# Attention and MLP on one core: a block takes the first 512 tokens of one batch, and the last block takes all eight 64-token tails

## The chip, the cores and the metric

One core of a Trainium2 chip runs the whole program. The metric is the device time of one execution in microseconds (us). Before the change it is 324.11 us (median of 3 runs, 323.73 to 324.36). The profile is of one execution; its span (322.6 us) leaves out about 1.7 us that the device time has.

Engine names: PE is TensorE (PEld its weight loads), DVE is VectorE, ACT is ScalarE, POOL is GpSimd, SP is SyncE, which issues most DMAs.

## The reference, cut to what matters

```python
# q, k, v: [8 batches, 8 heads, 576 tokens, 64]
scores = scale * q @ k^T;  ret = scores * Dmat          # causal, decay gamma_h ** (i - j)
x = (ret @ v) -> [8 * 576, 512]                         # tokens in order: 576 of batch 0, 576 of batch 1, ...
h = x @ w_in                                            # [4608, 2048]
g = 0.5 * h * (1 + tanh(c * (h + 0.044715 * h**3)))
return g @ w_out                                        # [4608, 512], float32
```

## The kernel before

A batch has 576 tokens: four chunks of 128 and a **tail** of 64. Attention is done chunk by chunk with a running state; its output lands in `xT`. The MLP (the two layers with `w_in` and `w_out`) works on **blocks** of 512 tokens, nine in all. Before the change, block t takes tokens 512t to 512t+511 of the running order, so block 1 needs the tail of batch 0, then 448 tokens of batch 1. The MLP's second layer is sixteen matmuls for each of four 128-token tiles in block 0, and in later blocks seven half-size products (a Strassen-like scheme, `prod`) with sums by VectorE (`act_sums`; the sums of the weights are `weight_sums`). Attention work for the next block is put between the MLP's steps at places written by hand: `at(block, step, work)`. Every engine runs its instructions in the order written. A **cast** is the copy of a loaded float32 tile to 16 bits (with a scaling for q and k); a **turn** is its transpose. TensorE writes its results to PSUM, a memory of eight banks. The code is cut ("..."), and most comments in it are mine.

```python
    def load_tail(b):                       # six small DMAs issued by POOL, 384 KB
        for key in "kqv":
            for u in range(2):
                load(b, key, NC, u)
...
    def turn_dma(b):                        # batches from NPE on: transposed by DMA
        a = att[b]
        for key in "kq":
            nc.sync.dma_start_transpose(out=a["t" + key], in_=a[key])
...
        def send(o, i):                     # output of a block: 128 rows, two tiles
            nc.sync.dma_start(
                out=out[TB * t : TB * t + TB, :].rearrange("(u i p) d -> p u i d", u=2, i=2)[:, :, i, :], in_=o
            )
...
        elif m == 4:
            if last:                        # the last two stores: 128 rows in one piece each
                add(keep["o1"][:, u, 0:HD], keep["s1"][:, u], pr("B")[:, u])
                r0 = TB * t + 256 * u + 128
                nc.sync.dma_start(out=out[r0 : r0 + 128, :], in_=keep["o1"][:, u])
...
    at(0, -4, lambda: load_tail(0))                                  # tail 0 inside block 0
    at(0, 8, lambda: [cc(0, key, NC, P) for key in "kqv"])           # its casts, on POOL
    for p in range(HP):
        at(0, 15 + p, lambda p=p: turn_q4(1, p, (A.copy, V.tensor_copy)[p % 2]))
    at(0, 19, lambda: turn(0, NC, A.copy))
...
        if t == 0:                          # second layer of block 0: two passes over w_out, two banks each
            for i0, tags in ((0, "AB"), (2, "CA")):
                ...
```

## Time and profile before

| | before |
|---|---|
| device time, median | 324.11 us |
| span of the profile | 322.6 us |
| TensorE busy | 305.2 us (95%) |
| last VectorE add ends; span ends 3.3 us later | 319.33 us |

The profile by stretches comes first. Each row has a start and an end in us from the span's start, its length, then busy us and number of instructions for each engine, the granted TensorE clock (1.00 is full), the share of the 16 DMA engines' time that is busy, and GB/s. The cuts are where TensorE starts the first layer of blocks 1, 2, 3 and 8.

```profile
36.00:62.40 26.40, 21.83 (x178) 10.56 (x175) 17.26 (x28) 8.06 (x16) 16.75 (x21) 1.00 1.10 238
62.40:99.40 37.00, 35.14 (x406) 28.74 (x405) 29.40 (x49) 23.00 (x46) 25.82 (x31) 1.00 1.11 221
99.40:134.60 35.20, 34.19 (x334) 22.27 (x332) 21.72 (x43) 18.71 (x37) 18.45 (x26) 1.00 0.99 192
134.60:292.00 157.40, 157.40 (x1415) 99.86 (x1414) 84.05 (x181) 84.15 (x162) 35.58 (x45) 1.00 0.54 111
292.00:322.60 30.60, 26.36 (x178) 17.07 (x175) 10.36 (x23) 10.72 (x18) 0.00 (x0) 1.00 0.18 70
```

TensorE has no gap in blocks 3 to 7 (row 4). It stands 4.6 us in the rest of block 0 (row 1), 1.9 us in block 1, 1.0 us in block 2. Row 1 also has a DMA share above 1: the queues are full. Who is waited for there is shown by the chain of waits (start, length, what; each piece is what released the next):

```profile
36.40 8.59 DMA ld<-in_q_dram
...
45.07 1.05 POOL cq L223
...
48.15 1.06 POOL ck L232
49.20 1.02 POOL cq L232
50.22 0.80 POOL cv L221
51.03 1.00 POOL ck L232
52.03 0.56 POOL cv L221
```

Batch 1's q arrives late (45 us), then POOL casts one tile after another. The three casts from 48.15 to 51.02 us are tail 0's.

### The profile page before, as it was taken

How to read it: one execution, taken by the hardware profiler on the slowest of the kernel's cores; microseconds unless marked ns; L12 is line 12 of the kernel's file. 1: busy time of each engine (PE TensorE's matmuls, PEld its weight loads, DVE VectorE, ACT ScalarE, POOL GpSimd, SP SyncE). 2: the span in 40 equal slices, each digit the busy share in tenths (PEclk: the TensorE clock that was granted, in tenths of full speed). 3: DMA queues.
4: the chain of work that ended last, by engine and by line, in shares of the span. 5: the costliest groups of instructions: out<-in, count | busy, mean ns of one | idle time of the engine just before them, and what ended most of it. 6: DMA issues, size and time to landing. Idle time of an engine off the chain costs nothing.

```text
span 322.6 us, 6913 instructions
## 1 busy us (share of the span) xinstructions
PE 305.2 (95%) x2785; PEld 199.3 (62%) x2785; DVE 183.6 (57%) x367; ACT 167.2 (52%) x322; POOL 124.9 (39%) x179
## 2 busy tenths in 40 slices
PE   6889967998999999999999999999999999999994
PEld 2458624676786458745864586458646864685483
DVE  5853467897874667564647463754467446633341
ACT  6466322696643665365537654665376237614700
POOL 8679339966754409600960096009100000000000
PEclk9799999999999999999999999999999999999999
DMA  8999999999999978995599689900820030003003
GB/s 197 223 347 384 291 271 216 208 247 250 197 202 205 206 202 158 201 197 166 127 218 183 194 152 200 236 2 3 185 93 0 2 131 2 2 0 130 2 0 132
DMA packets 123472, 51.31 MB, mean 159 GB/s; under 512 B 111920, under 2 KB 113968, under 8 KB 123440
## 3 DMA queue, kind: packets, MB, share of 16 engines
q1 hardware_dynamic: 121904, 47.72, 66.9%
q0 software_dynamic: 1536, 3.15, 4.6%
q8 instruction: 22, 0.36, 0.5%
q14 instruction: 10, 0.08, 0.1%
HBM read 36.70 MB, written 9.44 MB: 143 GB/s over the span
## 4 chain that ended last, share of the span: by engine, by line
PE 74%; DMA 10%; DVE 6%; SPq 4%; issue 2%; POOL 2%; ACT 1%; DVEq 0%; POOLq 0%
PE hp L389 31%; PE opB L476 13%; PE opC L476 9%; PE opA L476 8%; DMA ld<-in_moe_w_out_dram 4%; DMA ld<-in_moe_w_in_dram 3%; PE xs L337 3%; PE st L288 3%; SPq L90 3%; DMA ld<-in_q_dram 3%; PE us L307 2%; PE xs L355 2%; PE tr L262 1%; DVE ret L294 1%; DVE wt L447 1%
## 5 line engine op out<-in xcount | busy, mean ns | idle before, releaser
L389 PE MATMUL hp<-xT,w_in_sb 128*128 128x512 f16 x448 | 103.8, 379 | 0.0
L395 ACT ACTIVATE gT<-hp 128x512 f16<-128x512 f32 x112 | 67.1, 599 | 61.5 <-PE hp L389 61.1
L389 PEld LDWEIGHTS <-w_in_sb 128*128 128x128 f16 x448 | 41.6, 98 | 44.3 <-issue 0.5
L294 DVE TENSOR_TENSOR ret<-st,cm 128x512 f16<-128x512 f32 x64 | 41.2, 685 | 35.9 <-PE st L288 35.8
L476 PEld LDWEIGHTS <-gT 128*128 128x128 f16 x512 | 49.3, 98 | 7.5 <-issue 0.7
L476 PEld LDWEIGHTS <-s 128*128 128x128 f16 x384 | 36.6, 98 | 5.2 <-issue 0.5
L328 ACT CAST tbd<-ws 64x256 f16<-64x256 f32 x64 | 25.8, 403 | 24.6 <-DVE ws L323 23.9
L232 POOL TENSOR_TENSOR ck<-ld,sc 128x512 f16<-128x512 f32 x31 | 33.2, 1071 | 11.5 <-DMA ld<-in_k_dram 6.8
L476 PE MATMUL opB<-wt,gT 128*128 128x256 f16 x256 | 31.4, 273 | 0.5 <-DVE ost L490 0.5
L406 PE MATMUL hp<-xT,w_in_sb 128*128 128x256 f16 x256 | 30.3, 273 | 1.5 <-ACT gT L412 0.7
L476 PE MATMUL opA<-w_out_sb,gT 128*128 128x256 f16 x256 | 30.8, 273 | 0.0
L458 DVE TENSOR_TENSOR s<-gT 128x512 f16<-128x512 f16 x32 | 14.6, 456 | 25.9 <-ACT gT L395 24.9
L634 POOL COPY gate<-s 128x1 f16<-128x1 f16 x4 | 0.8, 188 | 69.5 <-DVE s L461 69.5
L406 PEld LDWEIGHTS <-w_in_sb 128*128 128x128 f16 x256 | 24.4, 98 | 5.1 <-POOL w_in_sb L532 1.5
L232 POOL TENSOR_TENSOR cq<-ld,sc 128x512 f16<-128x512 f32 x24 | 25.9, 1078 | 0.1
L412 ACT ACTIVATE gT<-hp 128x512 f16<-128x512 f32 x32 | 18.9, 596 | 9.5 <-PE hp L406 9.3
L490 DVE TENSOR_TENSOR ost<-k,opC 128x512 f32<-128x512 f32 x16 | 11.0, 687 | 18.4 <-PE opC L476 18.1
L376 ACT CAST xT<-xs 128x512 f16<-128x512 f32 x31 | 18.1, 583 | 2.0 <-PE xs L355 1.0
L288 PE MATMUL st<-tt 64*128 64x128 f16 x288 | 15.6, 221 | 3.3 <-DVE tt L266 1.4
L490 DVE TENSOR_TENSOR k<-k,opB 128x512 f32<-128x512 f32 x16 | 10.9, 683 | 12.7 <-PE opB L476 12.6
L288 PEld LDWEIGHTS <-tt 64*128 64x128 f16 x288 | 8.5, 95 | 15.5 <-issue 10.9
L337 PEld LDWEIGHTS <-cv 128*64 128x64 f16 x288 | 9.4, 110 | 13.9 <-issue 12.5
(87 smaller groups left out, 387.8 us busy)
## 6 DMA issues: line engine op xcount, KB each, us to landing
out_dram<-ost SPq DMA_DIRECT2D x17, 512.0 KB, 3.3
ld<-in_q_dram SPq DMA_DIRECT2D x32, 256.0 KB, 5.1
ld<-in_k_dram SPq DMA_DIRECT2D x32, 256.0 KB, 5.8
ld<-in_v_dram SPq DMA_DIRECT2D x32, 256.0 KB, 5.6
ld<-in_moe_w_in_dram SPq DMA_DIRECT2D x16, 256.0 KB, 5.8
ld<-in_moe_w_out_dram SPq DMA_DIRECT2D x16, 256.0 KB, 5.7
lt<-in_k_dram POOLq DMA_DIRECT2D x16, 64.0 KB, 4.9
lt<-in_q_dram POOLq DMA_DIRECT2D x16, 64.0 KB, 5.9
```

The lines of the kernel that those rows point to most:

```text
L232: eng.tensor_tensor(out=dst.rearrange("p (h d) -> p h d", d=D), in0=raw.rearrange("p (h d) -> p h d", d=D), in1=sc[:, s0 : s0 + nh].unsque ...
L288: nc.tensor.matmul(st[hl][:, 128 * p : 128 * p + 128], a["tk"][r, 4 * c + p, :], tq(b, c, p)[r], start=True, stop=True)
L294: nc.vector.tensor_tensor(out=r[:, 0:w], in0=st[hl][:, 0:w], in1=m.rearrange("p n i -> p (n i)"), op=ALU.mult)
L328: cp(out=tbd[b % 2][r, c, :, r], in_=att[b]["w"][r])
L337: nc.tensor.matmul(xs[64 * hl : 64 * hl + 64, 128 * p : 128 * p + 128], a["v"][:, col(c, p, hl)], a["ret"][c, hl][:, 128 * p : 128 * p + 128],
L376: nc.scalar.copy(out=xT[:, g0 : g0 + 2], in_=src)
L389: nc.tensor.matmul(hp.rearrange("p (g t) -> p g t", t=TL), w_in_sb[:, ct, 128 * fc : 128 * fc + 128], xT[:, o : o + TB // TL, ct, :], star ...
L395: nc.scalar.activation(out=gT[t][:, fc].rearrange("p i n -> p (i n)"), in_=hp, func=AF.Gelu_apprx_tanh)
L406: nc.tensor.matmul(hp[:, 256 * x : 256 * x + 256].rearrange("p (g t) -> p g t", t=TL), w_in_sb[:, ct, 128 * (f + x) : 128 * (f + x) + 128] ...
L412: nc.scalar.activation(out=gT[t][:, f : f + 2, 2 * u : 2 * u + 2, :].rearrange("p f i n -> p f (i n)"), in_=hp.rearrange("p (f n) -> p f n ...
L476: nc.tensor.matmul(op[tag][:, HD * u : HD * u + HD], lhs(f), rhs[:, f], start=(new and u == 0 and f == 0), stop=(f == NH - 1), skip_group_ ...
L490: nc.vector.tensor_tensor(out=o, in0=a, in1=b, op=ALU.add)
```

## The change

The intent: keep tail 0 out of the crowded blocks 0 and 1. Block b takes tokens 0 to 511 of batch b; block 8 takes the eight tails. So each tail may be done at any time before block 8, and its states (`tbt`) and turned operands (`ett`) are kept apart. The second layer of block 0 uses four PSUM banks, so that the second half can begin before all of w_out has come. Batch 3 is transposed by DMA and no longer by TensorE, all tails by TensorE, and from batch `HOLD` on the loads are held back until the transposes have been issued. The diff, cut to its core (comments mine):

```diff
-    NPE = 4
+    NPE = 3
+    HOLD = 3
...
         def send(o, i):
-            nc.sync.dma_start(
-                out=out[TB * t : TB * t + TB, :].rearrange("(u i p) d -> p u i d", u=2, i=2)[:, :, i, :], in_=o
-            )
+            if t < B:
+                nc.sync.dma_start(
+                    out=out[S * t : S * t + TB, :].rearrange("(u i p) d -> p u i d", u=2, i=2)[:, :, i, :], in_=o
+                )
+                return
+            for v in range(2):
+                end(o[:, v], i, v)
+        def end(o, i, v):
+            b = 4 * v + 2 * i
+            nc.sync.dma_start(out=out.rearrange("(b s) d -> b s d", s=S)[b : b + 2, M0:S, :], in_=o)
...
-                r0 = TB * t + 256 * u + 128
-                nc.sync.dma_start(out=out[r0 : r0 + 128, :], in_=keep["o1"][:, u])
+                end(keep["o1"][:, u], 1, u)
...
-    at(0, -4, lambda: load_tail(0))
-    at(0, 8, lambda: [cc(0, key, NC, P) for key in "kqv"])
-    at(0, 11, lambda: weight_sums(0))
+    at(0, 23, lambda: weight_sums(0))
     for p in range(HP):
-        at(0, 15 + p, lambda p=p: turn_q4(1, p, (A.copy, V.tensor_copy)[p % 2]))
-    at(0, 19, lambda: turn(0, NC, A.copy))   # and tail 0's score, av, put at 21, 24, 25
+        at(0, (20, 21, 22, 24)[p], lambda p=p: turn_q4(1, p, A.copy))
-    TU = [(0, 21), (0, 25), (0, 29), (1, 1)]          # batch 1: casts and turn in one place
+    CU = [(0, 6), (0, 7), (0, 30), (1, 0)]            # casts on their own, earlier
+    TU = [(0, 24), (0, 28), (0, 32), (1, 1)]
...
+    PLAN = {1: (8, 13, 18, 23), 2: (9, 14, 19, 24), ...}             # four chunks of batch t+1 in block t
+    TAILS = {0: ((1, 10), (2, 0), (2, 4)), 1: ((2, 5), (3, 0), (3, 4)), ..., 7: ((7, 3), (7, 10), (7, 14))}
...
-            for i0, tags in ((0, "AB"), (2, "CA")):
+            tags = ("A", "B", "C", "hp")
+            for i0, f0, f1 in ((0, 0, 12), (2, 0, 8), (0, 12, 16), (2, 8, 16)):
```

More of the change, by code (lines that the diff above doesn't have):

```diff
@@ L40 @@
     NH = NF // 2
-    W = NC * 512 + 256
+    W = NC * 512
     NB = W // 128
-    RX = 1536
-    NPE = 4
+    NPE = 3
     LD = 16
@@ L58 @@
     ctx.enter_context(tc.manual_schedule())
-    BUFS = {"hp": 2, "att": 3, "A": 1, "B": 1, "C": 1}
+    BUFS = {"hp": 2, "t0": 1, "t1": 1, "t2": 1, "A": 1, "B": 1, "C": 1}
+    turns = {"n": 0}
     def bank(tag, name, dt=F32):
+        if tag == "att":
+            tag = "t" + str(turns["n"] % 3)
+            turns["n"] += 1
         return ps.tile([128, 512 if dt == F32 else 1024], dt, tag=tag, name=name, bufs=BUFS[tag])
@@ L121 @@
         seq += body(b)
-    q_ld = {"next": 0, "free": LD}
+    q_ld = {"next": 0, "free": LD, "hold": False}
     def pump(freed=0):
         q_ld["free"] += freed
-        while q_ld["next"] < len(seq):
+        while q_ld["next"] < len(seq) and not q_ld["hold"]:
             s = seq[q_ld["next"]]
@@ L194 @@
     for i in range(2):
-        t = const.tile([128, NC, HP, 128], F16, name=f"tbd{i}")
-        tbd.append(t)
+        tbd.append(const.tile([128, NC - 1, HP, 128], F16, name=f"tbd{i}"))
+    tbt = [const.tile([128, HP, 128], F16, name=f"tbt{i}") for i in range(3)]
     w_in_sb = const.tile([128, 4, DF], F16, name="w_in_sb")
     w_out_sb = const.tile([128, NF, DM], F16, name="w_out_sb")
-    xT = const.tile([128, RX // TL, HP, TL], F16, name="xT")
+    GM, GT = 2 * (TB // TL), 2 * (TB // TL)
+    xT = const.tile([128, GM + B, HP, TL], F16, name="xT")
     def filler(n, tag="C"):
@@ L210, in new_casts, with new_tail, act_of, turned @@
             a[key] = sb.tile([128, W], F16, tag="c" + key, name="c" + key, bufs=2)
+    def new_tail(b):
+        a = att[b]
+        for key in "kqv":
+            a["e" + key] = sb.tile([128, 256], F16, tag="e" + key, name="e" + key, bufs=2)
+        a["ett"] = sb.tile([128, 2, 2, 128], F16, tag="ett", name="ett", bufs=2)
+    def act_of(b, key, c):
+        return att[b][key if c < NC else "e" + key]
+    def turned(b, c):
+        return (att[b]["tt"], 4 * c) if c < NC else (att[b]["ett"], 0)
     def cast(b, key, c, eng):
@@ L215, in cast @@
         raw = a["raw"].pop((key, c))[:, 0:w]
-        dst = a[key][:, 512 * c : 512 * c + w]
+        o = 512 * c if c < NC else 0
+        dst = act_of(b, key, c)[:, o : o + w]
         if key == "v":
@@ L260, in turn @@
             for i in range(n):
-                o = 512 * c + 128 * i
+                o = (512 * c if c < NC else 0) + 128 * i
                 nc.tensor.transpose(
-                    t[:, 128 * (n * y + i) : 128 * (n * y + i) + 128], a[key][:, o : o + 128], ident
+                    t[:, 128 * (n * y + i) : 128 * (n * y + i) + 128], act_of(b, key, c)[:, o : o + 128], ident
                 )
         m = len(keys)
+        d, o = turned(b, c)
         copy(
-            out=a["tt"][:, 0:m, 4 * c : 4 * c + n, :].rearrange("p y n t -> p y (n t)"),
+            out=d[:, 0:m, o : o + n, :].rearrange("p y n t -> p y (n t)"),
             in_=t[:, 0 : 128 * n * m].rearrange("p (y x) -> p y x", y=m),
@@ L274, in turn_dma @@
             nc.sync.dma_start_transpose(out=a["t" + key], in_=a[key])
+        q_ld["hold"] = False
+        pump()
     def tq(b, c, p):
-        t = att[b]["tq"]
-        return t[:, 4 * p + c, :] if b < NQ and c < NC else t[:, 4 * c + p, :]
+        d, o = turned(b, c)
+        return d[:, 1, 4 * p + c if b < NQ and c < NC else o + p, :]
     def score(b, c, tag="att"):
@@ L283, in score @@
         w = 128 * n
+        d, o = turned(b, c)
         st = [bank(tag, "st") for _ in range(2)]
@@ L288, in score @@
                 nc.tensor.matmul(
-                    st[hl][:, 128 * p : 128 * p + 128], a["tk"][r, 4 * c + p, :], tq(b, c, p)[r], start=True, stop=True
+                    st[hl][:, 128 * p : 128 * p + 128], d[r, 0, o + p, :], tq(b, c, p)[r], start=True, stop=True
                 )
@@ L299, in col @@
     def col(c, p, hl):
+        c = c % NC
         return slice(512 * c + 128 * p + 64 * hl, 512 * c + 128 * p + 64 * hl + 64)
@@ L327, in spread @@
             r = slice(64 * hl, 64 * hl + 64)
-            cp(out=tbd[b % 2][r, c, :, r], in_=att[b]["w"][r])
+            cp(out=(tbd[b % 2][r, c, :, r] if c < NC - 1 else tbt[b % 3][r, :, r]), in_=att[b]["w"][r])
     def av(b, c, tag="att"):
@@ L338, in av @@
                     xs[64 * hl : 64 * hl + 64, 128 * p : 128 * p + 128],
-                    a["v"][:, col(c, p, hl)],
+                    act_of(b, "v", c)[:, col(c, p, hl)],
                     a["ret"][c, hl][:, 128 * p : 128 * p + 128],
@@ L348, in av @@
                         xs[:, o : o + 64],
-                        td[:, NC - 1, 2 * u + s, :],
-                        a["tq"][:, 4 * NC + s, 64 * u : 64 * u + 64],
+                        tbt[b % 3][:, 2 * u + s, :],
+                        tq(b, c, s)[:, 64 * u : 64 * u + 64],
                         start=False, stop=True, skip_group_check=True,
@@ L361, in av @@
         a["xs"] = xs
-    NG = RX // TL
     def put(b, c):
         xs = att[b].pop("xs")
-        g0 = (b * S + 128 * c) // TL % NG
         if c == NC:
             nc.scalar.copy(
-                out=xT[:, g0].rearrange("p (u s) t -> p s u t", u=2),
+                out=xT[:, GM + b].rearrange("p (u s) t -> p s u t", u=2),
                 in_=xs[:, 0:256].rearrange("p (s u t) -> p s u t", s=2, u=2),
@@ L374, in put @@
         src = xs.rearrange("p (n g t) -> p g n t", n=HP, g=2)
-        if g0 + 1 < NG:
-            nc.scalar.copy(out=xT[:, g0 : g0 + 2], in_=src)
-        else:
-            for u in range(2):
-                nc.scalar.copy(out=xT[:, (g0 + u) % NG], in_=src[:, u])
+        g0 = 8 * (b % 2) + 2 * c
+        nc.scalar.copy(out=xT[:, g0 : g0 + 2], in_=src)
     gT = {}
@@ L386, in up @@
         hp = bank("hp", "hp")
-        o = TB * t // TL % NG
+        o = 8 * (t % 2) if t < B else GM
         for ct in range(4):
@@ L402, in up_half @@
         hp = bank("hp", "hp")
-        o = TB * t // TL % NG + 4 * u
+        o = (8 * (t % 2) if t < B else GM) + 4 * u
         for x in range(2):
@@ L555 @@
     nc.vector.memset(tbd[0], 0.0)
+    nc.vector.memset(tbt[0], 0.0)
     filler(8)
@@ L579 @@
         put(0, c)
+    PLAN = {1: (8, 13, 18, 23), 2: (9, 14, 19, 24), 3: (9, 14, 19, 24), 4: (9, 14, 19, 24), 5: (9, 14, 19, 24),
+            6: (10, 15, 19, 24)}
+    TAILS = {0: ((1, 10), (2, 0), (2, 4)), 1: ((2, 5), (3, 0), (3, 4)), 2: ((3, 5), (4, 0), (4, 4)),
+             3: ((4, 5), (5, 0), (5, 4)), 4: ((5, 5), (6, 0), (6, 3)), 5: ((6, 1), (6, 16), (7, 3)),
+             6: ((6, 17), (7, 2), (7, 8)), 7: ((7, 3), (7, 10), (7, 14))}
     gate = const.tile([128, 1], F16, name="gate")
@@ L589, in run @@
             f()
-    at(0, -12, lambda: nc.gpsimd.memset(tbd[1], 0.0))
-    at(0, -4, lambda: load_tail(0))
+    at(0, -12, lambda: [nc.gpsimd.memset(x, 0.0) for x in (tbd[1], tbt[1], tbt[2])])
     for f in range(NF):
@@ L600, with chunk, tail_in, tail_cast @@
         at(0, 2 + p, lambda p=p, e=e: cc(1, "q", p, e))
-    at(0, 8, lambda: [cc(0, key, NC, P) for key in "kqv"])
-    at(0, 11, lambda: weight_sums(0))
+    at(0, 23, lambda: weight_sums(0))
     for p in range(HP):
-        at(0, 15 + p, lambda p=p: turn_q4(1, p, (A.copy, V.tensor_copy)[p % 2]))
-    at(0, 19, lambda: turn(0, NC, A.copy))
-    at(0, 21, lambda: score(0, NC))
-    at(0, 24, lambda: av(0, NC))
-    at(0, 25, lambda: put(0, NC))
-    TU = [(0, 21), (0, 25), (0, 29), (1, 1)]
-    SU = [(0, 23), (0, 27), (0, 31), (1, 3)]
-    VU = [(0, 27), (0, 31), (1, 2), (1, 6)]
+        at(0, (20, 21, 22, 24)[p], lambda p=p: turn_q4(1, p, A.copy))
+    CU = [(0, 6), (0, 7), (0, 30), (1, 0)]
+    TU = [(0, 24), (0, 28), (0, 32), (1, 1)]
+    SU = [(0, 26), (0, 30), (1, 0), (1, 3)]
+    VU = [(0, 29), (0, 33), (1, 2), (1, 6)]
     for c in range(NC):
-        at(*TU[c], lambda c=c: (cc(1, "k", c, P), cc(1, "v", c, P), turn(1, c, A.copy)))
-        at(*SU[c], lambda c=c: (score(1, c, "hp" if c < 2 else "att"), state(1, c), scan(1, c)))
+        at(*CU[c], lambda c=c: (cc(1, "k", c, P), cc(1, "v", c, P)))
+        at(*TU[c], lambda c=c: turn(1, c, A.copy))
+        at(*SU[c], lambda c=c: (score(1, c), state(1, c), scan(1, c)))
         at(*VU[c], lambda c=c: (av(1, c), put(1, c), spread(1, c, A.copy)))
     at(1, 1, lambda: weight_sums(4))
-    def tail_casts(b, engs):
-        for key, e in zip("kqv", engs):
-            cc(b, key, NC, e)
+    def chunk(t, u, b, c):
+        if b < NPE or c == NC:
+            at(t, u - 2, lambda: turn(b, c, V.tensor_copy))
+        at(t, u, lambda: score(b, c))
+        if c < NC:
+            at(t, u, lambda: (state(b, c), scan(b, c)))
+            at(t, u + 2, lambda: spread(b, c, A.copy))
+        at(t, u + 3, lambda: av(b, c))
+        at(t, u + 4, lambda: put(b, c))
+    def tail_in(t, u, b):
+        at(t, u, lambda: load_tail(b))
+    def tail_cast(t, u, b):
+        at(t, u, lambda: (new_tail(b), [cc(b, key, NC, e) for key, e in zip("kqv", (P, P, A))]))
+    for t, us in PLAN.items():
+        for c, u in enumerate(us):
+            chunk(t, u, t + 1, c)
+    for b, (l, k, u) in TAILS.items():
+        tail_in(*l, b)
+        tail_cast(*k, b)
+        chunk(*u, b, NC)
     for b in range(2, B):
@@ L626 @@
         if b == 2:
-            t0, ut = 1, [1, 1, 1, 5, 5, 5, 9, 9, 9, 12, 12, 12]
-        elif b == 3:
-            t0, ut = 1, [16, 16, 17, 18, 19, 20, 21, 22, 23, 24, 25, 26]
+            t0, ut = 1, [1, 1, 2, 6, 6, 7, 11, 11, 12, 16, 16, 17]
         else:
@@ L632 @@
         at(t0, ut[0], lambda b=b: (new_casts(b), new_turned(b)))
-        if b >= 4:
+        if b >= HOLD:
+            at(t0, ut[0], lambda: q_ld.update(hold=True))
             at(t0, ut[0], lambda t=t0: nc.gpsimd.tensor_copy(out=gate, in_=gs[t]["4"][:, NH - 1, 1, 0:1]))
@@ L636 @@
             at(t0, u, lambda b=b, key=key, c=c, e=eng[key]: cc(b, key, c, e))
-        if b == 2:
-            at(0, 31, lambda: load_tail(1))
-            at(1, 9, lambda: tail_casts(1, (P, P, A)))
-            at(1, 12, lambda: load_tail(2))
-            at(1, 26, lambda: tail_casts(2, (P, P, A)))
-        else:
-            at(t0, ut[-1] if b == 3 else ut[0] - 1, lambda b=b: load_tail(b))
-            at(*((2, 14) if b == 3 else (t0, ut[-1] + 1)), lambda b=b: tail_casts(b, (P, P, A)))
-        if b >= NPE:
-            at(t0, ut[-1] + 2, lambda b=b: turn_dma(b))
-    todo = [(2, 0), (2, 1), (1, NC), (2, 2)] + [(b, c) for b in range(2, B) for c in CH][3:]
-    plan = {1: (7, 12, 15, 20), 2: (2, 7, 11, 17, 22), 3: (2, 7, 16, 22), 4: (1, 6, 11, 17, 22),
-            5: (2, 7, 12, 20), 6: (1, 6, 11, 17, 22), 7: (2, 7, 12, 20)}
-    for t, us in plan.items():
-        for u in us:
-            b, c = todo.pop(0)
-            if b < NPE:
-                at(t, u - 2, lambda b=b, c=c: turn(b, c, V.tensor_copy))
-            at(t, u, lambda b=b, c=c: score(b, c))
-            if c < NC:
-                at(t, u, lambda b=b, c=c: (state(b, c), scan(b, c)))
-                at(t, u + 2, lambda b=b, c=c: spread(b, c, A.copy))
-            at(t, u + 3, lambda b=b, c=c: av(b, c))
-            at(t, u + 4, lambda b=b, c=c: put(b, c))
-    assert not todo
+        if b >= NPE:
+            at(t0, ut[-1] + 1, lambda b=b: turn_dma(b))
     order = [(u, g) for u, g in ((0, 0), (0, 1), (1, 0), (1, 1), (0, 2), (1, 2), (0, 3), (1, 3))]
@@ L672 @@
         if t == 0:
-            for i0, tags in ((0, "AB"), (2, "CA")):
-                lag = 2 if i0 else 0
-                for f in range(NF):
-                    mm = [(0, f)] + [(1, g) for g in range(max(f - lag, 0), f - lag + 1 if f < NF - 1 else NF)]
-                    steps.append(lambda i0=i0, tags=tags, mm=mm: [
-                        down_mm(0, i0 + n, g, tags[n]) for n, g in mm
-                    ] and None)
-                steps.append(lambda i0=i0: store_pair(0, i0, (A.copy, V.tensor_copy)))
-        else:
-            def sums(f0, f1):
-                return lambda: act_sums(t, f0, f1)
+            tags = ("A", "B", "C", "hp")
+            for i0, f0, f1 in ((0, 0, 12), (2, 0, 8), (0, 12, 16), (2, 8, 16)):
+                for f in range(f0, f1):
+                    steps.append(lambda f=f, i0=i0: [down_mm(0, i0 + n, f, tags[i0 + n]) for n in range(2)] and None)
+                if f1 == NF:
+                    steps.append(lambda i0=i0: store_pair(0, i0, (A.copy, V.tensor_copy)))
+        else:
             for u in range(2 if t == 1 else 0):
```

## The prediction

> **What bounds the kernel now.** The page gives TensorE 305.2 us busy in a span of 322.6 (95%), at full clock. The per-stretch table shows it without a gap from 134.8 to 292.1 us (five blocks of about 31.5 us each). The visible idle time lies before: 4.6 us in 36.0–62.4 (second layer of block 0), 1.9 us in 62.4–99.4 (block 1), 1.0 us in 99.4–134.8 (block 2). The chain of waits names the reason: until 45 us it runs through DMA (w_in, w_out, then 8.6 us on batch 1's q), then through POOL casts to 52.6 us, three of which (3 us) belong to tail 0; from 58 to 73.7 us through VectorE, and TensorE then stands 1.4 us for a VectorE copy.
>
> **What the change does.**
> 1. Block 1 needs no tail 0. Its loads (31.2–35.2 us on POOL, 0.4 MB; at the 240–290 GB/s of that stretch about 1.5 us of DMA time, just ahead of w_out and q) leave the congested stretch; so do its three casts (about 3 us of POOL's chain) and two masks (0.74 us VectorE).
> 2. Block 0 on four banks: 40 second-layer matmuls (8.6 us) can run before batch 1's q is needed, against about 30, and none of the last four w_out tiles is needed in the first 8.6 us. TensorE stands 1.0 us for w_out and 3.3 us for batch 1's and tail 0's operands today; most of it should be filled.
> 3. Batch 3 goes from TensorE to DMA transposes; all tails go to TensorE. The instruction listing has 16 transposes fewer (112 to 96 with identity), at 0.055 us each: 0.9 us of TensorE, all on the critical path. VectorE loses four copies of 0.69 us and two more turn to ScalarE, which has room.
> 4. MLP, masks, states: unchanged. Blocks 3 to 7 hold 16 chunks and 7 tails instead of 17 and 5: +1 us there.
>
> **Sum.** End of block 0: from 62.4 to about 57 us. Block 1 then becomes bound by VectorE (wt sums, masks, states: the same work, 4.5 us sooner), so I keep about 5 us at its end (99.4 to about 94.5). Block 2: 35.4 to about 33 us, since batch 3 isn't transposed there and the remaining gaps shrink; -2.5 us. Blocks 3–7: +1 us. Last block unchanged at 30.5 us. Span about 316, time about **317.0 us** (-2.2%), range **313 to 321.5**. Chances: faster by over 2% 0.57, within 2% 0.41, slower 0.02.
>
> The Trainium skill, page "SBUF — State Buffer", section "Who interferes with whom", says a VectorE instruction with two SBUF inputs contends with POOL instructions that read SBUF. The trace agrees: the same 128x512 sum takes 0.42 us with POOL idle and 1.13–1.26 us at 85.6–89 us beside POOL casts.
>
> **What would show each step.** (1, 2) TensorE idle in the second layer of block 0 falls from 4.6 us to under 2; waits for w_out vanish; block 1's first layer starts near 57 us. (3) 96 identity transposes; batch 3's DMA transposes land before score of batch 3 in block 2 at about 103 us. (4) Stretch from block 3 to block 7's end 157 to 159 us.
>
> **What would make it wrong.** Batch 3's transposes come after eight POOL casts (8 us, gated on the last activation sums of block 1) and take about 10 us to land (4.9 + 2.8 us issue); if they land late, block 2 stalls by some us. VectorE's chain in block 1 may hold all that block 0 gained (then 320). If instead the short idle times hidden by pipelining vanish too, 314.

## More of the kernel before

The end of the program is in the timeline (start, length, engine, line, operation, and in brackets what ended the engine's idle time):

```profile
317.24 0.37 SPq L492 DMA_DIRECT2D out_dram<-ost  x1
317.37 0.42 DVE L490 TENSOR_TENSOR ost<-k,opB 128x256 f32<-128x256 f32 x1 [0.19 <-PE opB L476]
317.82 1.89 SPq L516 DMA_DIRECT2D out_dram<-ost  x2
318.91 0.42 DVE L490 TENSOR_TENSOR ost<-k,opB 128x256 f32<-128x256 f32 x1 [1.12 <-PE opB L476]
```

Three stores, 1.05 MB, leave in the last 5.4 us.

## The result, and the profile after

The changed kernel takes **338.58 us** (median of 4 runs, 337.82 to 342.92; the three fast ones 337.82, 337.97 and 339.19), against 324.09 us before (median of the 4 runs of the same rounds). The ratio is 1.044, with an interval of 1.041 to 1.047: clearly slower. (Ratios here are the mean time of one kernel's fast runs over that of the other's of the same rounds, so not quite the ratio of the medians.) Executions over 1.5% slower than the fastest of the same kernel are left out of the means. The result is correct. The span is 336.1 us.

The stretches after, cut at the same events (same columns as before):

```profile
36.00:56.80 20.80, 19.64 (x153) 10.70 (x151) 14.33 (x23) 8.00 (x16) 12.05 (x12) 1.00 0.99 248
56.80:95.30 38.50, 36.90 (x440) 29.86 (x440) 28.96 (x51) 24.15 (x47) 23.71 (x30) 1.00 1.15 226
95.30:127.70 32.40, 32.40 (x303) 20.49 (x302) 19.01 (x39) 18.61 (x36) 13.11 (x17) 1.00 1.05 176
127.70:286.40 158.70, 158.53 (x1426) 100.19 (x1424) 88.67 (x186) 84.78 (x164) 50.73 (x70) 1.00 0.62 123
286.40:336.10 49.70, 26.42 (x178) 17.09 (x176) 10.36 (x23) 10.73 (x18) 0.00 (x0) 0.80 0.11 43
```

Block 1 starts 5.6 us sooner, block 3 6.9 us sooner, block 8 5.6 us sooner. Of the 5.6 us in the first row 3.4 are idle time of TensorE (4.6 to 1.2 us); the other 2.2 are TensorE work that now stands in later rows (21.8 to 19.6 us, 25 matmuls fewer; block 1 has 34 more). Then the last row: 49.7 us in place of 30.6, with the same matmuls (x178) and the same 26.4 us of TensorE. The chain of waits doesn't name this loss: it ends with the last instruction, a VectorE add at 313.78 us. The timeline of the end has it:

```profile
311.70 9.71 SPq L519 DMA_DIRECT2D out_dram<-ost  x4
311.82 0.42 DVE L508 TENSOR_TENSOR ost<-k,opB 128x256 f32<-128x256 f32 x1 [0.18 <-PE opB L494]
313.36 0.42 DVE L508 TENSOR_TENSOR ost<-k,opB 128x256 f32<-128x256 f32 x1 [1.12 <-PE opB L494]
```

After it nothing computes for 22.3 us. The stretch from 316 to 336 us in the same table:

```profile
316.00:336.00 20.00, 0.00 (x0) 0.00 (x0) 0.00 (x0) 0.00 (x0) 0.00 (x0) 0.50 0.12 48
```

All that moves are four stores of 256 KB at 48 GB/s on average, with a DMA share of 0.12, which is two engines of sixteen (0.125). Before, the same 1.05 MB went at mostly 330 to 420 GB/s. The DMA view of the two ends shows it, each cut into 40 slices (the q1 line has the queue's packets, MB, and the packets' time as a share of the 16 engines' time); kernel before, 316 to 323 us:

```profile
GB/s 0 0 0 0 0 0 0 0 0 0 0 0 269 386 374 410 339 410 421 363 410 374 374 328 340 386 386 375 47 0 0 0 0 0 0 0 0 0 0 0
DMA packets 560, 1.05 MB, mean 150 GB/s; under 512 B 48, under 2 KB 48, under 8 KB 560
q1 hardware_dynamic: 560, 1.05, 39.3%
```

and the changed kernel, 311 to 336 us:

```profile
DMA  0001110111111111111111111111111111111100
GB/s 0 0 0 20 33 26 26 43 49 52 52 52 46 52 52 52 52 46 52 52 52 52 46 52 52 52 52 46 52 52 52 52 46 52 52 52 52 46 0 0
DMA packets 520, 1.05 MB, mean 42 GB/s; under 512 B 8, under 2 KB 8, under 8 KB 520
q1 hardware_dynamic: 520, 1.05, 11.4%
```

The packets are as large as before (512 of them are the 2 KB rows), so small packets aren't the reason. Nor are slow packets: 39.3% of 16 engines in 7 us are 44.0 us of engine time before, and 11.4% of 16 in 25 us are 45.6 us after. In sum the packets took about as long as before; fewer engines worked at once. SyncE's 9.71 us for the four issues aren't the limit either: they are over at 321.4 us, and the bytes move at the same rate on to 335 us. The clock of 0.50 in this stretch, which pulls the span's mean to 0.965, isn't either: TensorE is done, and its clock was 1.00 until the last matmul.

### The profile page after: what moved, and what is told of

It is laid out like the page before. It is cut to its first block, busy times and chain, and to the rows that moved or that the text cites. A ratio compares the mean times of both kernels' runs of the same rounds, so it can differ in the third digit from the quotient of the medians.

```text
span 336.1 us, 6843 instructions
## 1 busy us (share of the span) xinstructions
PE 303.3 (90%) x2769; PEld 198.6 (59%) x2769; DVE 181.9 (54%) x367; ACT 168.3 (50%) x323; POOL 124.6 (37%) x181
## 4 chain that ended last, share of the span: by engine, by line
PE 81%; DVE 6%; DMA 4%; ACT 1%; issue 1%; SPq 1%; POOL 0%; DVEq 0%
PE hp L407 30%; PE opB L494 12%; PE opC L494 8%; PE opA L494 8%; PE hp L424 6%; PE op L443 4%; PE st L311 4%; PE xs L361 3%; DMA ld<-in_moe_w_in_dram 2%; PE us L331 2%; PE xs L379 2%; DMA ld<-in_k_dram 1%; PE tr L281 1%; DVE ret L317 1%; DVE wt L465 1%
## 5 line engine op out<-in xcount | busy, mean ns | idle before, releaser
L494 PE MATMUL opA<-w_out_sb,gT 128*128 128x256 f16 x256 | 31.6, 273 | 0.0
L352 ACT CAST tbd<-ws 64x256 f16<-64x256 f32 x48 | 19.3, 401 | 23.9 <-DVE ws L347 23.5
L476 DVE TENSOR_TENSOR s<-gT 128x512 f16<-128x512 f16 x32 | 13.5, 423 | 30.9 <-ACT gT L413 30.1
L347 DVE TENSOR_TENSOR ws<-vs,gt 128x256 f32<-128x256 f32 x24 | 16.0, 666 | 1.2
L311 PE MATMUL st<-tt 64*128 64x128 f16 x256 | 13.7, 221 | 2.9 <-DVE tt L286 1.2
L533 ACT COPY ost<-opA 128x512 f32<-128x512 f32 x8 | 4.7, 586 | 22.9 <-PE opA L494 22.9
```

What stands on the lines that cost most here:

```text
L311: nc.tensor.matmul(st[hl][:, 128 * p : 128 * p + 128], d[r, 0, o + p, :], tq(b, c, p)[r], start=True, stop=True)
L347: nc.vector.tensor_tensor(out=w, in0=uc, in1=gt, op=ALU.mult)
L352: cp(out=(tbd[b % 2][r, c, :, r] if c < NC - 1 else tbt[b % 3][r, :, r]), in_=att[b]["w"][r])
L494: nc.tensor.matmul(op[tag][:, HD * u : HD * u + HD], lhs(f), rhs[:, f], start=(new and u == 0 and f == 0), stop=(f == NH - 1), skip_group_ ...
```

## The experiments

My theory (A): the store's destination is `out[b:b+2, 512:576, :]`, whose slowest dimension is 2, and so only two DMA engines work. The Trainium skill, page "DMA: Bandwidth & Descriptors", section "Why a DMA increments its semaphore by 16 and not by 1", states the rule under "How many engines (k)": of the slowest dimension (over 1) of each side, the largest k up to 16 that divides both sizes is the number of engines. Here the sides have 128 partitions and 2 batches, so k = 2; the 0.12 share and 51 GB/s agree. Rivals: (B) pieces of 64 rows 1.2 MB apart are slow to write; (C) each store at the queue's end has a fixed cost of some 5 us.

### rows64: each store split in two, one for each batch

```diff
-            nc.sync.dma_start(out=out.rearrange("(b s) d -> b s d", s=S)[b : b + 2, M0:S, :], in_=o)
+            for j in range(2):
+                r0 = S * (b + j) + M0
+                nc.sync.dma_start(out=out[r0 : r0 + TL, :], in_=o[TL * j : TL * j + TL])
```

> The changed kernel with each of its last four stores (two batches of 64 rows, destination with outermost dimension 2) split into two stores of 64 rows of one batch: same rows, same bytes, eight stores instead of four. Theory A (such a store runs on only 2 of the 16 DMA engines, because its destination's slowest dimension is 2): the time from the last VectorE add to the end of the span falls from 22.3 us to 3.3 to 4 us as in the kernel before, so the span is about 317.4 us and the time about 319 us (ratio to before 0.98 to 0.99). Theory B (64-row pieces 1.2 MB apart are slow to write in HBM): no change, about 338 us. Theory C (each store costs some 5 us of fixed time at the end of the queue, one after the other): eight stores make it slower, about 355 us.

Measured: 321.41 us median (6 runs), ratio 0.989 (0.983 to 0.995); correct. The end after the last add falls from 22.3 to 6.0 us (314.13 to 320.1). B and C fall: the same scattered rows, in twice as many stores, are fast. But the end isn't as short as I expected (3.3 to 4 us). SyncE needs 5.02 us for eight issues, and the last one ends 3 us after the last add. The trace has a second reason, though: the bytes went at only some 205 GB/s with the DMA engines mostly 0.8 to 0.9 busy. They took 45.2% of 16 engines in 10 us, 72 us of engine time against 44 before. (The timeline, and the q1 line of the DMA view from 311 to 321 us.)

```profile
312.04 5.02 SPq L521 DMA_DIRECT2D out_dram<-ost  x8
313.71 0.42 DVE L508 TENSOR_TENSOR ost<-k,opB 128x256 f32<-128x256 f32 x1 [1.12 <-PE opB L494]
q1 hardware_dynamic: 640, 1.05, 45.2%
```

### rows64_two_queues: every second of these eight issued by ScalarE

```diff
-                nc.sync.dma_start(out=out[r0 : r0 + TL, :], in_=o[TL * j : TL * j + TL])
+                (nc.scalar if j else nc.sync).dma_start(out=out[r0 : r0 + TL, :], in_=o[TL * j : TL * j + TL])
```

> As rows64, with every second one of the eight last stores issued by ScalarE, which is idle there, instead of SyncE. Theory A: the end shortens by one or two issues (0.35 us each), so 0.3 to 0.7 us below rows64, about 318.5 us; it would be the fastest of all. B and C: about 338 us for B; about half of rows64's excess for C.

Measured: 319.81 us median (6 runs), ratio 0.982 (0.977 to 0.987), on the same chip as rows64. The end is 4.8 us (312.98 to 317.8): 1.2 us off, where I expected 0.3 to 0.7. That issuing was part of rows64's end is likely but not shown: the engine time of the stores fell too, from 72 to 54 us, and no run separates the two. Another 1.1 us of the difference between the two profiles comes from before block 1 (it starts at 55.93 against 57.02 us), where both kernels have the same instructions. It is scatter, and means that about 1 us in the start of block 1 between two single profiles is no evidence.

### before_two_row_blocks: the kernel before with only the stores' form

```diff
-                nc.sync.dma_start(out=out[r0 : r0 + 128, :], in_=keep["o1"][:, u])
+                end(keep["o1"][:, u], 1, u)      # end() and send() of the last block as in the changed kernel
```

> The kernel before, with the stores of its last block alone sent in the changed kernel's form (two batches of 64 rows, outermost dimension 2). The rows are the wrong ones, so the result is wrong on purpose; the arithmetic and the bytes are those of before. If the form of the stores is the whole loss, whatever else changed: the end after the last add grows from 3.3 to about 22 us at about 51 GB/s and the time to about 343 us. If the loss needs the changed order of work (rival): about 324 us.

Measured: 343.19 us median (4 runs), ratio 1.056. Its output is wrong, which doesn't matter for the time. The end is 22.5 us (318.57 to 341.1) at 49 to 52 GB/s for most of it:

```profile
316.48 10.07 SPq L493 DMA_DIRECT2D out_dram<-ost  x4
318.15 0.42 DVE L490 TENSOR_TENSOR ost<-k,opB 128x256 f32<-128x256 f32 x1 [1.12 <-PE opB L476]
```

The form of the stores alone (with four in place of three), and none of the changed order of work, makes the whole loss.

### store_forms: the stores by themselves

```diff
+    def fresh():                      # one buffer: the memset waits until the store before has landed
+        t = sb.tile([128, DM], F32, tag="t", name="t", bufs=1)
+        nc.vector.memset(t, 1.0)
+        return t
+    for n in range(3):
+        nc.sync.dma_start(out=out[1152:1280, :], in_=fresh())              # L45
+        nc.sync.dma_start(out=rows[0:2, 512:576, :], in_=fresh())          # L47; rows = out as (b s) d -> b s d
+        nc.sync.dma_start(out=rows[0:4, 512:544, :], in_=fresh())          # L49
+        nc.sync.dma_start(out=rows[0:8, 512:528, :], in_=fresh())          # L51
+        nc.sync.dma_start(out=r32[0:16, 256:264, :], in_=fresh())          # L53; r32 = 16 groups of 288 rows
+        nc.sync.dma_start(out=rows[0:2, 512:576, :].rearrange("b s d -> s b d"), in_=fresh())   # L55
+        ...                                                                # L57, L58: two of 64 rows
```

> No real kernel and a wrong result on purpose: stores of the same 256 KB tile by themselves, each waiting for the one before, three times round, with seven forms of the destination: 128 rows in a block; outermost dimension 2 (64 rows each), 4 (32 rows), 8 (16 rows), 16 (8 rows), all scattered; the same scattered rows as form 2 with the 64 rows outermost and the 2 batches inside; two stores of 64 rows. Theory A, with 25.6 GB/s an engine as the changed kernel's end shows (51 GB/s on two): about 2 us fixed plus 10.2 us for 2, 5.1 for 4, 2.6 for 8, 1.3 for 16, and 64 outermost as fast as the block (about 3 us). Theory B (scatter): all five scattered forms alike, about 10 us, the 64-outermost too. Theory C: all alike.

Measured, second round, in the timeline. The bracket of each memset has the wait of VectorE for the store above it:

```profile
34.66 0.35 SPq L45 DMA_DIRECT2D out_dram<-t  x1
36.92 0.48 DVE L40 MEMSET t<- 128x512 f32 x1 [2.28 <-DMA out_dram<-t]
37.43 0.58 SPq L47 DMA_DIRECT2D out_dram<-t  x1
45.43 0.48 DVE L40 MEMSET t<- 128x512 f32 x1 [8.03 <-DMA out_dram<-t]
45.94 0.58 SPq L49 DMA_DIRECT2D out_dram<-t  x1
52.06 0.48 DVE L40 MEMSET t<- 128x512 f32 x1 [6.15 <-DMA out_dram<-t]
52.58 0.60 SPq L51 DMA_DIRECT2D out_dram<-t  x1
56.78 0.48 DVE L40 MEMSET t<- 128x512 f32 x1 [4.24 <-DMA out_dram<-t]
57.30 0.57 SPq L53 DMA_DIRECT2D out_dram<-t  x1
60.35 0.48 DVE L40 MEMSET t<- 128x512 f32 x1 [3.08 <-DMA out_dram<-t]
60.86 0.57 SPq L55 DMA_DIRECT2D out_dram<-t  x1
63.49 0.48 DVE L40 MEMSET t<- 128x512 f32 x1 [2.66 <-DMA out_dram<-t]
64.01 0.49 SPq L57 DMA_DIRECT2D out_dram<-t  x1
64.55 0.59 SPq L58 DMA_DIRECT2D out_dram<-t  x1
67.16 0.48 DVE L40 MEMSET t<- 128x512 f32 x1 [3.18 <-DMA out_dram<-t]
```

The three rounds agree to 0.1 us. 256 KB take 8.0 us with 2 as the slowest dimension, 6.2 with 4, 4.2 with 8, 3.1 with 16. The decisive pair is L47 and L55: the same 128 rows in HBM, once with the 2 batches outermost (8.03 us), once with the 64 rows outermost (2.66 us). That rules out B again, and C. My numbers in the expectation were too large: I wrote 10.2 us of transfer for two engines, but 256 KB at 51 GB/s are 5.1 us. With 5.1, 2.6, 1.3 and 0.6 us the rest is 2.9, 3.6, 2.9 and 2.5 us, so the time falls with the number of engines, but not exactly as bytes over engines. The packet records of the second round show why. The packets move for 6.2, 4.4, 2.4 and 1.3 us, with 2.1, 3.7, 7.2 and 12.6 of them under way on average; that is k = 2, 4, 8 and 16 nearly as the page has it. The remaining 1.8 us is the same for each. The 128 packets together take 12.9 to 17.3 us of engine time in these four forms, against 11.1 us in L55. The two half tiles (L57, L58) take 18.3 us: stores of half the partitions cost DMA time here too, as in rows64. Why is open.

### interleaved_tails: k = 16 without more stores

```diff
+    tails = xT[:, GM : GM + B].rearrange("p g h t -> p (g h t)").rearrange(
+        "p (j h t b) -> p j h t b", j=B // 2, h=HP, b=2
+    )
-                out=xT[:, GM + b].rearrange("p (u s) t -> p s u t", u=2),
+                out=tails[:, b // 2, :, :, b % 2].rearrange("p (u s) t -> p s u t", u=2),
-                xT[:, o : o + TB // TL, ct, :],
+                xT[:, o : o + TB // TL, ct, :] if t < B else tails[:, :, ct].rearrange("p j t b -> p j (t b)"),
-            nc.sync.dma_start(out=out.rearrange("(b s) d -> b s d", s=S)[b : b + 2, M0:S, :], in_=o)
+            nc.sync.dma_start(out=out.rearrange("(b s) d -> s b d", s=S)[M0:S, b : b + 2, :], in_=o)
```

> The changed kernel with the tail tokens of two batches interleaved in the last block (ScalarE writes them so; no instruction is added), so that the four last stores keep their number, size and rows, but have the 64 rows as outermost dimension and the two batches inside. By theory A they run on 16 engines; with four issues instead of rows64's eight the end after the last add is 3.3 to 3.8 us, against 6.0 in rows64 and 22.3 in the changed kernel. Span about 317.3 us, time about 319 us, ratio 0.980 to 0.986, at or under rows64_two_queues. If the scattered rows were what is slow: about 338 us.

Measured: 318.38 us median (5 runs), ratio 0.982 (0.979 to 0.985); correct. The end is 3.5 us (313.35 to 316.8). Four issues take 2.66 us, and the bytes go at 340 to 410 GB/s. The timeline, and the DMA view from 311 to 317 us:

```profile
311.26 2.66 SPq L522 DMA_DIRECT2D out_dram<-ost  x4
312.93 0.42 DVE L511 TENSOR_TENSOR ost<-k,opB 128x256 f32<-128x256 f32 x1 [1.12 <-PE opB L497]
```

```profile
GB/s 0 0 0 0 0 0 0 0 0 0 137 410 396 410 341 369 410 396 341 383 410 382 355 410 383 396 341 410 301 14 0 0 0 0 0 0 0 0 0 0
q1 hardware_dynamic: 576, 1.05, 46.0%
```

The stores take 44 us of engine time (46.0% of 16 engines in 6 us), as in both kernels. This version is the changed kernel as it was meant, and it beats both kernels. The following ones ask which of its parts earns the gain.

### block0_in_pairs: interleaved_tails without the four banks

The edit puts the two passes of the kernel before (`((0, "AB"), (2, "CA"))`) back in block 0.

> interleaved_tails with the second layer of block 0 as before: two passes over all 16 tiles of w_out, two banks each. If the four banks carry the gain in block 0 (my prediction's step 2): TensorE idle between 36 and 62 us rises from 1.2 us to 3 or more and block 1 starts 2 to 3 us later; part of it reaches the end, time 1 to 3 us above interleaved_tails. If taking tail 0 out of blocks 0 and 1 carries it: within 0.7 us of interleaved_tails.

Measured: 318.38 us median (4 runs, same chip), ratio 0.981: the same as interleaved_tails. Block 1 starts at 56.69 us (56.22 with four banks, within the scatter), and TensorE doesn't wait for w_out in block 0 in either. The four banks earn nothing that these runs show.

### batch3_on_tensor: interleaved_tails with `NPE = 4`, `HOLD = 4`

> interleaved_tails with batch 3 transposed on TensorE again (32 transposes, 1.8 us by 0.055 us each, with four VectorE copies in block 2) instead of by DMA, and the loads held from batch 4 on. If TensorE bounds block 2 and the DMA transposes come in time: block 2 takes 32.3 + 1.8 = 34.1 us and the time is 1.8 us above interleaved_tails. If the early DMA transposes cost as much as they save: within 0.5 us.

Measured: 321.0 us median (4 runs, same chip), ratio 0.989. Block 2 takes 34.41 us against 32.32: 2.1 us, a little over the 1.8 us of the transposes alone. The other stretches from block 3 on are within 0.2 us of their length; block 1 (37.92 against 38.60) gives back most of what a start 0.9 us later took. So taking batch 3 off TensorE, with the loads held for it (the edit undoes both), is worth about 2 us.

### before_four_banks: the kernel before with the four banks alone

The edit puts the four-bank loop into the kernel before, and batch 1's first two scores into the attention banks.

> The kernel before with the second layer of block 0 on four banks alone (and batch 1's first two scores in the attention banks, as the changed kernel has it); tails, batch 3 and stores as before. By my prediction's steps 1 and 2 the gain in block 0 needs both the banks and tail 0's removal: 1 to 2 us off 324, the chain still passing POOL's three tail casts. If the banks alone do it: 4 us or more off. If VectorE's chain in block 1 takes it all: within 0.5 us of before.

Measured: 327.06 us median (6 runs), ratio 1.007 (1.004 to 1.010): about 2.3 us slower, outside all three expectations. Block 1 starts at 64.43 us against 62.40. With q's transposes at their old places, TensorE stands 1.8 us for the cast of q and 2.1 us behind VectorE's copy of a transpose, which the trace shows after the wt sums. Right after these stands, from about 53 to 57 us, the granted clock was 0.5 for 3.4 us, which the kernel before doesn't have there: four 128x512 matmuls took 1.91 us in place of 1.03. So part of the loss is likely the clock, and the run doesn't weigh the banks by themselves.

### old_order_no_tail and before_new_order: tail 0 or the order

The change in block 0 has two parts left: tail 0 is gone, and batch 1's casts, transposes and scores stand at other places. The first kernel is block0_in_pairs with the old places; the second is the kernel before, tail 0 kept, with the new places. The diff is cut to its core: `weight_sums(0)`, the scores (`SU`, and their banks) and `VU` go along.

```diff
 # old_order_no_tail; before_new_order has the reverse in the kernel before
-        at(0, (20, 21, 22, 24)[p], lambda p=p: turn_q4(1, p, A.copy))
-    CU = [(0, 6), (0, 7), (0, 30), (1, 0)]
-    TU = [(0, 24), (0, 28), (0, 32), (1, 1)]
+        at(0, 15 + p, lambda p=p: turn_q4(1, p, (A.copy, V.tensor_copy)[p % 2]))
+    TU = [(0, 21), (0, 25), (0, 29), (1, 1)]
```

> block0_in_pairs with batch 1's casts, transposes, scores and the wt sums of block 0 at the places in the order that the kernel before gives them; what is left of the change in block 0 is that tail 0 is not loaded, cast or computed there. If tail 0's removal carries block 0's gain (my prediction's step 1): TensorE starts block 1 by 58.5 us. If the later places of batch 1's operations in TensorE's order carry it: at 60.5 us or later, with waits of TensorE for casts between 42 and 53 us as in the kernel before, and the time about 3 us over block0_in_pairs.

> The complement: the kernel before, tail 0 still in block 0, with batch 1's casts, transposes, scores and wt sums at the changed kernel's places (its k and v casts of two chunks stand ahead of tail 0's casts on POOL). If the places carry the gain: TensorE starts block 1 at about 58 to 59 us instead of 62.4 and the time falls to about 320 to 321 us. If tail 0's removal carries it: block 1 starts at 61 us or later, time about 323 to 325 us.

Measured: old_order_no_tail 320.18 us (4 runs), ratio 0.985, block 1 from 59.11 us: between the two expectations. Against 62.40 before and 56.69 in block0_in_pairs, tail 0's removal brings 3.3 us and the order another 2.4 us (single profiles, with the scatter of about 1 us). Idle time of TensorE is 1.6 us of the first and 1.9 us of the second (4.6, then 2.9, then 1.1 us after 36 us); the rest is TensorE work that moved to later blocks. By the end of block 1 the order has kept 1.5 us of it (96.11 against 94.62). Without tail 0, POOL starts batch 1's first q cast at 42.41 us; before, at 45.07 us.

before_new_order is 335.53 us (4 runs), ratio 1.034, far from both expectations. Its longest waits of TensorE between 36 and 73 us (waiting operation, releaser, us in total, times, longest):

```profile
PE tr L262 <- POOL ck L232: 6.5, 1, 6.5
PE tr L262 <- DVE ret L294: 2.5, 1, 2.5
```

My edit put two chunks' casts ahead of tail 0's on POOL, but left tail 0's transposes ahead of batch 1's on TensorE. TensorE stood 6.5 us (46.4 to 52.9) for tail 0's casts, with batch 1's q cast and waiting behind them from 48.6 us on. And again the granted clock was lower around a stand: it was 0.5 from about 48.6 to 58.8 us, and for another 3.4 us after the second wait. So this run doesn't weigh the order by itself, as I had meant; it shows that the new places are bad with tail 0's operations left where they were.

## Why the prediction was wrong, point by point

| step | predicted | measured in the changed kernel |
|---|---|---|
| block 1 starts (62.4 before) | about 57 us | 56.8 |
| block 2 starts (99.4 before) | about 94.5 us | 95.3 |
| block 2 takes (35.2 before) | about 33 us | 32.4 |
| blocks 3 to 7 take (157.4 before) | 157 to 159 us | 158.7 |
| **last block (30.6 before)** | **unchanged, 30.5 us** | **49.7 us** |
| span | 316 us | 336.1 us |

The step that failed is "Last block unchanged at 30.5 us". Its arithmetic is unchanged: from block 8's first matmul to the last add 27.4 us pass in both kernels. But the step leaves out that the stores became others: I counted the bytes and rows of the last stores, which are the same, and not the form of their destination. Stores with 2 as the slowest dimension ran on two engines; the end went from 3.3 to 22.3 us, 19.0 us. The sum closes: 5.5 us gained up to the last add, 19.0 us lost after it, and 336.1 - 322.6 = 13.5. before_two_row_blocks makes the loss alone, and interleaved_tails takes it away alone, so this cause is shown. The diff and the skill page were both at hand; the division would have given k = 2, and as an estimate 1.05 MB at two sixteenths of the 330 to 420 GB/s before take 20 to 25 us.

With the stores mended, the rest came out 1.4 us worse than predicted (318.4 against 317.0 us). 0.7 us of this is a slip: I added 1.0 us to the span where the device time has 1.7. The span is 0.8 us over mine. That the sum comes so close is partly luck, since the reasons in it don't all hold.

Of the reasons inside the gain:

- Step 1 was right and too small. Tail 0's removal brings 3.3 us at block 1's start (1.6 of it idle time), and POOL starts on q 2.7 us sooner, where I had put 1.5 us of DMA time.
- Step 2 was wrong in its cause. What fills most of the gap that tail 0 leaves (2.9 to 1.1 us) is that batch 1's operations stand later in the order, with TensorE's work ahead of them; the four banks add nothing with it that shows (block0_in_pairs), and the kernel with them alone is 2.3 us slower (before_four_banks).
- Step 3 was right for batch 3: 2.1 us in block 2 for its 32 transposes. Its own sum, 0.9 us for 16 fewer, counts the tails' 16 more, which no run weighs. The DMA transposes of batch 3 were issued from 88.3 us on, and TensorE waited for none of them in block 2; my fear that they would be late didn't come true.
- That block 1 becomes bound by VectorE isn't shown. It takes 38.5 us in place of 37.0, but TensorE's work in it grew by 1.8 us (35.1 to 36.9), its idle time fell from 1.9 to 1.6 us, and VectorE's busy time fell from 29.4 to 29.0 us. TensorE's longest wait in it is again for a VectorE copy (1.2 us). So block 1's end near the predicted time (95.3 against 94.5 us) is right by the number, for another reason.

## What to carry to other kernels

When a change moves what a DMA writes, read the destination's dimensions from slowest to fastest, not just bytes and contiguous runs: a slowest dimension of 2 leaves two of sixteen engines at work. Look above all at the last stores, since nothing runs beside them and the chain of waits ends before them; a low DMA share (0.12 here) with large packets and no engine busy is the sign. A layout chosen upstream (tokens of two batches interleaved) can give the store a long outermost dimension for no added instruction, and is better here than more and smaller stores (an end of 3.5 us against 6.0), which paid in issue time, in the DMA engines' time, or in both.

## What the Trainium skill lacked or had wrong

- "DMA: Bandwidth & Descriptors", "How many engines (k)": right, and it would have saved the prediction. The runs show 51 GB/s on two engines, 25.6 GB/s each; the page's Specifications say about 27 GiB/s, which is 29 GB/s, so the runs stay 12% under it.
- The same page: no issue time by the form of a store on this chip that I found. In store_forms SyncE takes 0.34 to 0.38 us for 128 adjacent rows, and 0.49 to 0.68 us for the six other forms; eight such issues were 5.02 us at the end of rows64. In the changed kernel, with the stores before still moving, the four issues took 0.52 to 4.73 us each.
- The same page, "Rules for kernel authors", advises against two transfers to disjoint partition halves. The runs agree and give a size: an end of 6.0 us with halves, 3.5 us with whole tiles, and 72 us of the DMA engines' time against 44.
- "Perfetto Trace Analysis", "Identifying the Most-Contended Engine", says that 16 DMA engines make occupancy misleading, and goes by HBM utilization for DMA. In the last 22 us of the changed kernel neither is high: the DMA share is 0.12 at 48 GB/s, and yet the stores bound the program, with two engines' worth of packets under way. The page names specific DMA engines among the things that can bind; that a share near k/16 is how this looks is not on it.
- "SBUF — State Buffer", "Who interferes with whom", as quoted in the prediction: the trace agrees (0.42 us for a sum with POOL idle, 1.13 to 1.26 us beside POOL's casts).
